# Linear attention and an ELU layer: two scratch buffers for the denominators' discarded products

## The chip, the cores and the metric

The kernel runs on one core of a Trainium2 chip. A core has five engines with a queue of instructions each: TensorE (PE in the profile; its loading of stationary weights is PEld), VectorE (DVE), ScalarE (ACT), GpSimd (POOL) and SyncE (SP), which here issues all the DMA transfers. Each engine works through its queue in the order in which it was written; across engines, and where one instruction has to see that an earlier one is through, semaphores hold an instruction back. The metric is the device time of one execution in microseconds; the median of several executions is given.

## The reference

```python
# q, k, v: (8, 8, 576, 64); omega: (128, 64), all float32
scale = 1 / sqrt(sqrt(64))
def phi(x):                                   # x already times scale
    proj = einsum('bhsd,md->bhsm', x, omega)
    h = proj - sum(x * x, axis=-1, keepdims=True) / 2
    return exp(h - max(h, axis=-1, keepdims=True)) / sqrt(128)
q_p, k_p = phi(q * scale), phi(k * scale)
kv  = einsum('bhsm,bhsd->bhmd', k_p, v)
z   = sum(k_p, axis=2)
num = einsum('bhsm,bhmd->bhsd', q_p, kv)
den = einsum('bhsm,bhm->bhs', q_p, z)[..., None] + 1e-6
x   = (num / den), laid out as 4608 tokens of 512
h   = x @ w_in                                # w_in (512, 2048), float64
g   = where(h > 0, h, exp(min(h, 0)) - 1)
out = (g @ w_out).astype(float32)             # w_out (2048, 512), float64
```

The change touches two things of it: how `den` is computed, and where two float32 copies of `omega` lie.

## The kernel before

The attention works on 32 pairs of heads (8 batches of 4 pairs). A pair is loaded (`load_pair`), its keys and queries are projected and exponentiated (`project`), the key-value product and the key sums are formed (`kv`), and `finish` divides the queries' features by the denominators and multiplies them by the key-value product. The first 8 pairs are "native": they are projected in float32 straight against a tile `of` of 128 x 128, whose upper half is omega transposed times -scale and whose lower half is a constant that multiplies the squares of x (line 491). The other 24 are split into a high and a low float32r part and projected against `om`, which is made once from a second float32 copy of omega, `omf` (lines 399 to 405).

The two layers behind the attention run beside it. The tokens go in blocks of 384 through `layer1` (lines 969 to 971) and `layer2` (lines 1003 to 1005), while the float64 weights are converted on VectorE, ScalarE and GpSimd (lines 891 to 923) in the first two hundred microseconds. The last 1536 tokens go through another, seven-product form (`wide1`, `wide2`) when the attention is over; its weights are prepared by `prepare` and `prepare2`.

All this is written as some thousands of tasks with an engine, an estimated duration, a due time, and the buffers each reads and writes (`Plan.op`). A planner (`Plan.order`) replays them by its own estimates, gives each engine the ready task with the earliest due time, and so fixes the order of the queues before anything runs. A `Buf` has a tag and a number of slots; buffers with one tag take turns in these slots, and the planner lets a task start only if a slot is free. On the chip, the first instruction that writes a buffer waits by semaphore until those that used its slot before are through.

The denominators of a pair are made in `finish` on VectorE, by lines 726 to 730: for each of 9 rows of 128 tokens, one `tensor_tensor_reduce` multiplies the query features by the key sums, which lie in PSUM as `pz`, and sums the product along its row into a column of `den`. The sum is all that is wanted; the product itself, 128 x 128 numbers, goes into a buffer `junk` that nobody reads. They come in three tasks per pair: two groups of four products, and a third one of two products on 64 partitions each (the ninth row belongs half to one head and half to the other). The planner counts 210 ns for each product. The profile shows one such product as two instructions, CUSTOM_DVE_ANT_0 and DVE_READ_ACCUMULATOR2_ANT. Line 555, in `project`, uses the same operation to add the two parts of a projection and take its minimum; its output is wanted and goes into different parts of the features `h`.

The buffer `junk` is a `Buf` with one slot, made anew for every product and not listed with the planner. The buffer for the key sums, tag `zs`, has one slot of 128 x 256 numbers. `omf` is in that slot first, and the sums of pairs 8 to 31 follow (lines 616 to 640). `of` has a place of its own for the whole kernel.

Of the kernel before, what the change touches and what calls it, by code (L numbers as in the profile page):

```python
# [9 lines left out]
F32 = mybir.dt.float32  # L10
# [8 lines left out]
P = 128  # L19
# [286 lines left out]
def act(n, psum=False, ptr=False):  # L306
    return (51 if psum else 93) + 0.833 * n + (93 if ptr else 0)
# [11 lines left out]
def performer_elu_kernel(  # L319
# [26 lines left out]
    make_identity(nc, ident)  # L346


    of = const.tile([P, M], F32, name="of")
    om = const.tile([P, 2 * M], F32R, name="om")  # L350
    nc.vector.memset(of[D:P], 0.5 * SCALE * SCALE)


    ones = const.tile([P, P], F32R, name="ones")
# [32 lines left out]
            nc.vector.tensor_scalar(x, x, -SCALE, None, ALU.mult)  # L387

    def omega(due):
        op("SP", 500, due + 0.005, lambda: nc.sync.dma_start(of[0:D], omT), (), ("of",), D * M * 4)  # L390
        op(
            "ACT", act(M), due + 0.1, lambda e: times(e, of[0:D]), ("of",), ("of",),
            alt=[("DVE", dve(M, True), 0.0)], port=True,
        )
        t = Buf(sb, [P, M], F32, "zs", "omf", 1)
        due += 15
        for a in range(2):
            r = slice(a * D, a * D + D)
            op("SP", 500, due, lambda r=r: nc.sync.dma_start(t()[r], omT), (), ((t, a),), D * M * 4)
        both = ((t, 0), (t, 1))  # L400
        op("ACT", act(M), due + 2, lambda e: times(e, t()), both, both, alt=[("DVE", dve(M, True), 0.0)], port=True)
        op("DVE", dve(M), due + 3, lambda: nc.vector.tensor_copy(om[:, 0:M], t()), ((t, 0), (t, 1)), ("oh",))
        op(
            "DVE", dve(M), due + 4,
            lambda: nc.vector.tensor_tensor(om[:, M:], t(), om[:, 0:M].bitcast(F32), ALU.subtract),
            ((t, 0), (t, 1), "oh"), ("om",),
        )
# [43 lines left out]
    def project(i, nm, due):  # L451

        s = st[i]
        x = s["x" + nm]
        h = s["h" + nm] = Buf(sb, [P, NJ, M], F32, "h", f"h{nm}_{i}", 4)
        nb = small("nb" + nm, NJ, f"nb{nm}_{i}")

        def exps(g, js, src, due, reads):
            def f():
                for j in js:  # L460
                    nc.scalar.activation(  # L461
                        h()[:, j, :], src(j), AF.Exp, bias=nb()[:, j:j + 1], scale=-1.0
                    )
            op("ACT", len(js) * act(M, native(i, nm), True), due, f, (*reads, (nb, g)), ((h, g),))

        if native(i, nm):
            for a in range(2):
                def square(e, a=a):
                    if e == "ACT":
                        nc.scalar.activation(x()[D:P, a], x()[0:D, a], AF.Square)  # L470
                    else:
                        tt(e, x()[D:P, a], x()[0:D, a], x()[0:D, a], ALU.mult)

                op(
                    "ACT", act(S), due - 3 + a, square, ((x, a),), ((x, a, 2),),
                    alt=other("sq", "POOL", pool(S), "DVE", dve(S)), port=True,
                )
            for g in range(3):
                d = due + 2.2 * g
                p = bank(i, "acc%d" % g, f"pp{nm}_{i}_{g}")  # L480
                n = 4 if g < 2 else 1
                js = slice(4 * g, 4 * g + n)

                def mms(g=g, p=p):
                    for c in range(4 if g < 2 else 2):
                        t, a = 2 * g + c // 2, c % 2
                        if g < 2:
                            o = p()[:, c * M:(c + 1) * M]
                        else:
                            o = p()[a * D:a * D + D, 0:M]  # L490
                        nc.tensor.matmul(o, x()[:, a, t * P:min(t * P + P, S)], of, start=True, stop=True)

                def view(p=p):
                    return p().rearrange("p (j x) -> p j x", j=4)

                op("PE", 872 if g < 2 else 240, d, mms, [*((x, a, 2) for a in range(2)), "of"], (p,))
                op(
                    "DVE", 66 + n * 133, d + 1,
                    lambda js=js, n=n, view=view: nc.vector.tensor_reduce(nb()[:, js], view()[:, 0:n], AX.X, ALU.min),
                    (p,), ((nb, g),),  # L500
                )
                exps(g, range(js.start, js.stop), lambda j, g=g, view=view: view()[:, j - 4 * g], d + 1.5, (p,))
            return

        def t():
            return x()[:, 1].rearrange("p (j d) -> p j d", d=D)

        op(
            "ACT", act(S), due - 4,
            lambda: nc.scalar.activation(t(), t(), AF.Square, scale=SCALE * 0.5**0.5), ((x, 3),), ((x, 3),),  # L510
        )
        sq = small("sq" + nm, NJ, f"sq{nm}_{i}")
        op("DVE", dve(S), due - 3, lambda: nc.vector.tensor_reduce(sq(), t(), AX.X, ALU.add), ((x, 3),), (sq,))

        y = Buf(sb, [P, 2 * S], F32R, "t", f"t{nm}_{i}", 2)
        for a in range(2):
            r, o = slice(a * D, a * D + D), slice(D - a * D, P - a * D)
            cs = slice(a * S, a * S + S)  # L520
            parts = ((x, 0),)
            op(
                "ACT", act(S), due - 5 + a, lambda e, r=r, cs=cs: copy(e, y()[r, cs], x()[r, 0]), parts, ((y, a, "h"),),
                alt=other("y_hi", "DVE", dve(S, True)), port=True,
            )
            op(
                "POOL", pool(S), due - 4 + a,
                lambda e, r=r, o=o, cs=cs: tt(e, y()[o, cs], x()[r, 0], y()[r, cs].bitcast(F32), ALU.subtract),
                (*parts, (y, a, "h")), ((y, a, "l"),), alt=other("y_lo", "DVE", dve(S)), port=True,
            )  # L530
        for c in range(5):
            d = due + 1.1 * c
            p = Buf(ps, [P, 512], F32, "pa", f"pp{nm}_{i}_{c}", 3)
            p2 = Buf(sb, [P, 2, M], F32, "p2", f"p2{nm}_{i}_{c}", 4)
            n = 2 if c < 4 else 1
            g = 0 if c < 2 else 1

            def mms(c=c, p=p, n=n):
                for a in range(n):
                    o = a * (S + D) + c * P  # L540
                    nc.tensor.matmul(p()[:, a * 256:(a + 1) * 256], y()[:, o:o + P], om, start=True, stop=True)  # L541

            def view(p=p):
                return p().rearrange("p (a x) -> p a x", a=2)

            op("PE", mm(256, n), d, mms, [(y, a, z) for a in range(2) for z in "hl"] + ["oh", "om"], (p,))
            op(
                "ACT", act(n * M, True), d + 0.5, lambda e, n=n, p2=p2, view=view: copy(e, p2()[:, 0:n], view()[:, 0:n, M:]),
                (p,), (p2,), alt=other("p2", "DVE", dve(n * M)),
            )  # L550

            def ttr(c=c, n=n, p2=p2, view=view):
                for a in range(n):
                    j = 2 * c + a
                    nc.vector.tensor_tensor_reduce(
                        out=h()[:, j, :], in0=view()[:, a, 0:M], in1=p2()[:, a, :], scale=1.0, scalar=LARGEST,
                        op0=ALU.add, op1=ALU.min, accum_out=nb()[:, j:j + 1],
                    )

            op("DVE", n * 212, d + 1, ttr, (p, p2), ((h, g, c), (nb, g, c)))  # L560
            if c in (1, 4):
                js = range(0, 4) if c == 1 else range(4, NJ)

                def bias(js=js):
                    m, q = nb()[:, js.start:js.stop], sq()[:, js.start:js.stop]
                    nc.gpsimd.tensor_tensor(m, m, q, ALU.add)
                    nc.gpsimd.tensor_tensor(m, m, q, ALU.subtract)  # L567

                op("POOL", 2 * pool(4), d + 1.3, bias, [sq, *((nb, g, e) for e in range(5))], ((nb, g),))
                exps(g, js, lambda j: h()[:, j, :], d + 1.5, [(h, g, e) for e in range(5)])  # L570
# [118 lines left out]
    def finish(i, due):  # L689
# [25 lines left out]
        for g in range(3):  # L715
# [7 lines left out]

            def dens(slots=slots):
                for j, a, r in slots:
                    junk = Buf(sb, [P, M], F32, "junk", f"junk_{i}_{j}_{a}", 1)
                    nc.vector.tensor_tensor_reduce(  # L727
                        out=junk()[r], in0=h()[r, j, :], in1=pz()[r, a * P:(a + 1) * P], scale=1.0, scalar=EPS,
                        op0=ALU.mult, op1=ALU.add, accum_out=den()[r, j:j + 1],
                    )  # L730
# [971 lines left out]
```

## Time and profile before

| | |
|---|---|
| median of 3 runs | 1024.42 us (1021.78 to 1025.25) |
| the profiled execution | 1023.41 us |
| its span, first to last instruction | 1021.6 us |
| granted TensorE clock, mean | 0.998 of full |
| TensorE, VectorE, ScalarE, GpSimd busy | 97%, 84%, 75%, 55% |
| denominators on VectorE (line 727, product) | 320 products, 90.4 us |
| their sums' reads (line 727) | 320, median 81 ns |

A busy TensorE is not TensorE at its peak, since matmuls are pipelined and their ends are modelled. Times of single instructions are in microseconds from the span's start. An engine's next instruction may start while the one before it is still on record, because the engine takes in new data while it is emptying; so the distance from start to start says what an instruction costs its queue, rather than its recorded duration. "Idle before" names what ended a wait, as inferred from the semaphores. The chain of waits follows the work that ended last back through what released each step.

### The profile page before, as it was taken

The numbers are of one execution on the slowest core, as the hardware profiler recorded it, in microseconds if no ns is written. First come the engines' busy times: TensorE is split into PE (matmuls) and PEld (weight loads), VectorE is DVE, ScalarE is ACT, GpSimd is POOL, SyncE is SP. The second block draws the span as 40 slices with busy tenths as digits, with TensorE's granted clock in tenths as the row PEclk, the third lists the DMA queues.
The fourth block names the chain that finished last, engine by engine and source line by source line (L and its number), as shares of the span: only waits on it lengthen the run. The fifth ranks groups of instructions, "written<-read, shape, count | busy, mean of one in ns | idle before, by whom it ended". The sixth has DMA issues, their size and how long they took to land.

```text
span 1021.6 us, 24319 instructions
## 1 busy us (share of the span) xinstructions
PE 988.5 (97%) x7806; PEld 887.3 (87%) x7806; DVE 856.6 (84%) x3077; ACT 767.9 (75%) x2064; POOL 559.0 (55%) x745
## 2 busy tenths in 40 slices
PE   8889999989999999999999999999999999999997
PEld 7777889878888888888888888887888999999997
DVE  5899978886778968887889888889999989779766
ACT  6888866876668888788887878785545788877774
POOL 1566666766546676676667776785442232223221
PEclk9999999999999999999999999999999999999999
DMA  7555777767766767676775767665787885775762
GB/s 201 153 178 187 231 254 256 243 213 240 238 218 222 231 203 229 200 229 198 245 227 183 238 194 234 203 224 209 261 306 275 304 294 176 237 235 193 229 198 70
DMA packets 93264, 226.27 MB, mean 221 GB/s; under 512 B 23056, under 2 KB 35024, under 8 KB 93136
## 3 DMA queue, kind: packets, MB, share of 16 engines
q1 hardware_dynamic: 93136, 224.70, 67.7%
q8 instruction: 63, 1.03, 0.4%
q14 instruction: 65, 0.53, 0.2%
HBM read 187.43 MB, written 37.22 MB: 220 GB/s over the span
## 4 chain that ended last, share of the span: by engine, by line
PE 64%; DVE 18%; ACT 7%; DMA 6%; issue 3%; POOL 1%; SPq 1%; DVEq 0%; ACTq 0%; POOLq 0%
PE acs L1512 8%; PE ph L969 6%; PE ph L971 6%; PE ph L970 6%; PE acc L1003 6%; PE A L1354 6%; PE acc L1005 6%; PE acc L1004 6%; PE B L1354 4%; DVE junk L727 3%; PE pkv L609 3%; PE ppq L541 2%; PE pn L829 2%; PE ppk L541 2%; DMA w1c<-w1s 1%
## 5 line engine op out<-in xcount | busy, mean ns | idle before, releaser
L969 PE MATMUL ph<-xh,w1c 128*128 128x384 f32 x512 | 177.2, 346 | 6.9 <-DVE g L990 4.9
L970 PE MATMUL ph<-xl,w1c 128*128 128x384 f32 x512 | 172.6, 337 | 1.2 <-DVE xl L794 1.2
L971 PE MATMUL ph<-xh,w1c 128*128 128x384 f32 x512 | 172.5, 337 | 0.0
L1003 PE MATMUL acc<-w2h,g 128*128 128x512 f32 x384 | 154.7, 403 | 0.1
L1005 PE MATMUL acc<-w2h,g 128*128 128x512 f32 x384 | 151.6, 395 | 0.0
L1004 PE MATMUL acc<-w2l,g 128*128 128x512 f32 x384 | 151.4, 394 | 0.0
L969 PEld LDWEIGHTS ph<-xh,w1c 128*128 128x128 f32 x512 | 96.4, 188 | 19.5 <-DVE g L990 9.7
L727 DVE CUSTOM_DVE_ANT_0 junk<-hq,pz 128x128 f32<-128x128 f32 (+1 forms) x320 | 90.4, 282 | 22.1 <-PE pz L705 10.3
L381 POOL TENSOR_TENSOR hq<-hq,den 128x512 f32<-128x512 f32 (+1 forms) x96 | 80.8, 850 | 36.6 <-DVE den L736 32.0
L970 PEld LDWEIGHTS ph<-xl,w1c 128*128 128x128 f32 x512 | 96.4, 188 | 4.2 <-DVE xl L794 1.6
L978 ACT ACTIVATE e<-ph 128x384 f32<-128x384 f32 x128 | 62.7, 489 | 47.3 <-PE ph L971 46.6
L971 PEld LDWEIGHTS ph<-xh,w1c 128*128 128x128 f32 x512 | 96.4, 188 | 0.0
L982 DVE SCALAR_TENSOR_TENSOR ph<-e,ph 128x384 f32<-128x384 f32 x128 | 71.2, 556 | 25.0 <-ACT e L979 24.2
L381 POOL TENSOR_TENSOR gq<-yh,gq 128x256 fp32r<-128x256 f32 x49 | 42.5, 868 | 86.5 <-ACT gq L376 76.3
L1005 PEld LDWEIGHTS acc<-w2h,g 128*128 128x128 f32 x384 | 72.1, 188 | 17.2
L1003 PEld LDWEIGHTS acc<-w2h,g 128*128 128x128 f32 x384 | 72.2, 188 | 16.0 <-issue 6.3
L381 POOL TENSOR_TENSOR tk<-xk,tk 64x576 fp32r<-64x576 f32 x45 | 64.1, 1425 | 31.8 <-ACT tk L376 16.8
L461 ACT ACTIVATE hq<-hq,nbq 128x128 f32<-128x128 f32 x216 | 68.5, 392 | 16.4 <-POOL nbq L567 16.0
L1004 PEld LDWEIGHTS acc<-w2l,g 128*128 128x128 f32 x384 | 72.3, 188 | 8.7
L461 ACT ACTIVATE hk<-hk,nbk 128x128 f32<-128x128 f32 x216 | 68.4, 392 | 15.0 <-POOL nbk L567 14.7
L381 POOL TENSOR_TENSOR tq<-xq,tq 64x576 fp32r<-64x576 f32 x46 | 65.8, 1431 | 19.6 <-ACT tq L376 8.2
L990 DVE TENSOR_TENSOR g<-ph,g 128x384 fp32r<-128x384 f32 x128 | 70.5, 550 | 6.0 <-PE pn L829 2.2
(222 smaller groups left out, 2827.3 us busy)
## 6 DMA issues: line engine op xcount, KB each, us to landing
w1c<-w1s SPq DMA_DIRECT2D x112, 512.0 KB, 4.4
wp<-w1t SPq DMA_DIRECT2D x48, 512.0 KB, 3.9
raw_w<-in_w_dram SPq DMA_DIRECT2D x32, 512.0 KB, 4.1
xk<-in_kx_dram SPq DMA_DIRECT2D x24, 576.0 KB, 4.5
xq<-in_qx_dram SPq DMA_DIRECT2D x24, 576.0 KB, 4.5
wp<-w1s SPq DMA_DIRECT2D x24, 512.0 KB, 4.1
v<-in_v_dram SPq DMA_DIRECT2D x32, 325.0 KB, 3.1
w1s<-w1c SPq DMA_DIRECT2D x16, 512.0 KB, 4.0
```

Of the source, the lines that this page charges most:

```text
L381: (nc.vector if e == "DVE" else nc.gpsimd).tensor_tensor(*args)
L461: nc.scalar.activation(h()[:, j, :], src(j), AF.Exp, bias=nb()[:, j:j + 1], scale=-1.0)
L727: nc.vector.tensor_tensor_reduce(out=junk()[r], in0=h()[r, j, :], in1=pz()[r, a * P:(a + 1) * P], scale=1.0, scalar=EPS, op0=ALU.mult, op1 ...
L969: nc.tensor.matmul(ph(), wh, xh[:, c, o:o + TB], start=(c == 0), stop=False)
L970: nc.tensor.matmul(ph(), wh, xl[:, c, o:o + TB], start=False, stop=False)
L971: nc.tensor.matmul(ph(), wl, xh[:, c, o:o + TB], start=False, stop=(c == NC - 1))
L982: lambda: nc.vector.scalar_tensor_tensor(ph(), e(), -1.0, ph(), ALU.add, ALU.max), (p, e), (p,),
L1003: nc.tensor.matmul(a(), g[0]()[:, ts], w2h[:, f], start=(f == f0), stop=False)
L1004: nc.tensor.matmul(a(), g[0]()[:, ts], w2l[:, f], start=False, stop=False)
L1005: nc.tensor.matmul(a(), g[1]()[:, ts], w2h[:, f], start=False, stop=(f == f1 - 1))
L1354: nc.tensor.matmul(o, at(a, i), u[b][:, i], start=(start and fresh_bank and i == 0 and n == 0), stop=(i == 1 and n == 2), skip_group_check ...
L1512: nc.tensor.matmul(bank()[:, z * TH:(z + 1) * TH], g()[:, a * TH + z * P:a * TH + z * P + P], w(b), start=(j == 0 and z == 0 and m == 0), ...
```

## The change

The buffer for the discarded products gets two slots instead of one, so that one product is written to one slot and the next to the other. The room for the second slot (512 bytes per partition) comes from `of`: it is no longer a place of its own but the first user of the key sums' slot, tag `zs`. `omf`, which was there before, takes one of the slots of `junk`. The tasks keep their engines, estimated durations and due times; `of` is named as a buffer to the planner where it was named by a string.

```diff
-    of = const.tile([P, M], F32, name="of")
+    of = Buf(sb, [P, M], F32, "zs", "of", 1)
     om = const.tile([P, 2 * M], F32R, name="om")
-    nc.vector.memset(of[D:P], 0.5 * SCALE * SCALE)
+    nc.vector.memset(of()[D:P], 0.5 * SCALE * SCALE)
...
     def omega(due):
-        op("SP", 500, due + 0.005, lambda: nc.sync.dma_start(of[0:D], omT), (), ("of",), D * M * 4)
+        op("SP", 500, due + 0.005, lambda: nc.sync.dma_start(of()[0:D], omT), (), (of,), D * M * 4)
         op(
-            "ACT", act(M), due + 0.1, lambda e: times(e, of[0:D]), ("of",), ("of",),
+            "ACT", act(M), due + 0.1, lambda e: times(e, of()[0:D]), (of,), (of,),
             alt=[("DVE", dve(M, True), 0.0)], port=True,
         )
-        t = Buf(sb, [P, M], F32, "zs", "omf", 1)
+        t = Buf(sb, [P, M], F32, "junk", "omf", 2)
...
-                        nc.tensor.matmul(o, x()[:, a, t * P:min(t * P + P, S)], of, start=True, stop=True)
+                        nc.tensor.matmul(o, x()[:, a, t * P:min(t * P + P, S)], of(), start=True, stop=True)
...
-                op("PE", 872 if g < 2 else 240, d, mms, [*((x, a, 2) for a in range(2)), "of"], (p,))
+                op("PE", 872 if g < 2 else 240, d, mms, [*((x, a, 2) for a in range(2)), of], (p,))
...
             def dens(slots=slots):
                 for j, a, r in slots:
-                    junk = Buf(sb, [P, M], F32, "junk", f"junk_{i}_{j}_{a}", 1)
+                    junk = Buf(sb, [P, M], F32, "junk", f"junk_{i}_{j}_{a}", 2)
                     nc.vector.tensor_tensor_reduce(
                         out=junk()[r], in0=h()[r, j, :], in1=pz()[r, a * P:(a + 1) * P], scale=1.0, scalar=EPS,
```

## Rows read from the trace of the kernel before

**Rows 1.** The page: busy us, share, instructions per engine; then the chain by engine.

```profile
PE 988.5 (97%) x7806; PEld 887.3 (87%) x7806; DVE 856.6 (84%) x3077; ACT 767.9 (75%) x2064; POOL 559.0 (55%) x745
...
PE 64%; DVE 18%; ACT 7%; DMA 6%; issue 3%; POOL 1%; SPq 1%; DVEq 0%; ACTq 0%; POOLq 0%
```

**Rows 2.** Stages: stretch, length; PE, PEld, DVE, ACT, POOL busy (instructions); clock, DMA.

```profile
22.00:125.00 103.00, 94.13 (x679) 78.65 (x679) 94.88 (x330) 87.93 (x237) 64.93 (x57) 1.00 0.60 189
125.00:300.00 175.00, 169.09 (x1091) 147.96 (x1091) 135.96 (x428) 124.95 (x303) 111.84 (x132) 1.00 0.71 234
300.00:725.00 425.00, 421.11 (x3620) 366.49 (x3618) 363.03 (x1690) 338.79 (x943) 294.62 (x448) 1.00 0.69 220
```

**Rows 3.** Chain of waits by line, 22 to 125 us, then 300 to 725 us.

```profile
by line: DVE junk L727 14.1%; issue 7.9%; DVE u_w L914 7.6%; DVE nbk L499 6.8%; ACT hq L461 5.7%; DVE u_w L902 5.6%; DVE nbq L499 5.2%; DVE u_w L909 5.1%; DVE xl L794 4.1%; DMA w1s<-w1c 3.8%; DVE qh L378 3.0%; DVE xq L381 2.5%; DVE ph L982 
...
by line: PE ph L969 10.1%; PE acc L1003 9.9%; PE ph L971 9.4%; PE ph L970 9.4%; PE acc L1005 9.3%; PE acc L1004 9.3%; PE pkv L609 5.4%; PE ppq L541 4.8%; PE pn L829 4.6%; PE ppk L541 4.0%; DVE junk L727 3.3%; DMA w1c<-w1s 1.9%; issue 1.4%; 
```

**Rows 4.** Line 727: duration min/median/max in ns, first and last start in us.

```profile
L727 DVE CUSTOM_DVE_ANT_0 junk<-hq,pz x320: 244/286/292, 22.6 to 724.2; 128x128 f32<-128x128 f32 x128, 64x128 f32<-64x128 f32 x32
...
L727 DVEq EVENT_SEMAPHORE  x31: 21/21/50, 23.0 to 111.3; - x31
```

**Rows 5.** VectorE in order of time from 404.5 us: start, duration, line, operation.

```profile
404.52 0.29 DVE L727 CUSTOM_DVE_ANT_0 junk<-hq,pz 128x128 f32<-128x128 f32 x1 [1.75 <-PE pz L705]
404.74 0.08 DVE L727 DVE_READ_ACCUMULATOR2_ANT den<- 128x1 f32 x1
404.85 0.29 DVE L727 CUSTOM_DVE_ANT_0 junk<-hq,pz 128x128 f32<-128x128 f32 x1
...
405.73 0.08 DVE L727 DVE_READ_ACCUMULATOR2_ANT den<- 128x1 f32 x1
405.73 0.28 DVE L555 CUSTOM_DVE_ANT_0 hq<-ppq,p2q 128x128 f32<-128x128 f32 x1
...
405.94 0.28 DVE L555 CUSTOM_DVE_ANT_0 hq<-ppq,p2q 128x128 f32<-128x128 f32 x1
```

**Rows 6.** VectorE in order of time from 88.3 us, a native pair's denominators.

```profile
88.36 0.08 DVE L727 DVE_READ_ACCUMULATOR2_ANT den<- 128x1 f32 x1
88.58 0.29 DVE L727 CUSTOM_DVE_ANT_0 junk<-hq,pz 128x128 f32<-128x128 f32 x1
```

**Rows 7.** VectorE in order of time from 69.9 us, a pair's third group.

```profile
69.93 0.07 DVE L727 DVE_READ_ACCUMULATOR2_ANT den<- 64x1 f32 x1
70.04 0.29 DVE L727 CUSTOM_DVE_ANT_0 junk<-hq,pz 64x128 f32<-64x128 f32 x1
70.26 0.08 DVE L727 DVE_READ_ACCUMULATOR2_ANT den<- 64x1 f32 x1
70.37 0.69 DVE L499 TENSOR_REDUCE nbq<-ppq 128x4 f32<-128x512 f32 x1
```

**Rows 8.** Stages, line 727 alone: stretch, length, VectorE busy (records of two instructions).

```profile
22.00:125.00 103.00, 23.25 (x160) 1.00 0.60 189
...
300.00:725.00 425.00, 60.93 (x420) 1.00 0.69 220
```

**Rows 9.** ScalarE's waits, 22 to 125 us: waiter, releaser, us in total, times, longest.

```profile
ACT hk L461 <- DVE nbk L499: 6.8, 7, 1.6
```

**Rows 10.** Users of the moved buffers: duration in ns, first and last start in us.

```profile
L491 PE MATMUL ppq<-of,xq x160: 272/275/377, 18.2 to 110.7; 128*128 128x128 f32 x128, 128*64 128x128 f32 x32
...
L405 DVE TENSOR_TENSOR om<-omf,om x1: 282/282/282, 16.0 to 16.0; 128x128 fp32r<-128x128 f32 x1
...
L625 POOL TENSOR_TENSOR zs<-hk x24: 725/738/1140, 138.2 to 689.1; 128x256 f32<-128x256 f32 x24
```

**Rows 11.** Weight loads: issues of the page (us to landing); chain; TensorE behind it.

```profile
w1c<-w1s SPq DMA_DIRECT2D x112, 512.0 KB, 4.4
...
718.18 8.04 DMA w1c<-w1s
...
726.36 0.41 PE L969 MATMUL ph<-xh,w1c 128*128 128x384 f32 x1 [1.53 <-DMA w1c<-w1s]
```

## The prediction

> **What bounds the kernel now.** I read the page first, then a table of busy time by stage, then the chain of waits in the same stages, and last the order of single VectorE instructions. The page shows TensorE busy for 97% of the span and VectorE for 84%, while the chain that ended last runs 18% of the span through VectorE [rows 1]. Line 727 computes the denominators. The averages hide that there are three regimes [rows 2]. From 22 to 125 us (eight "native" pairs beside the weight conversion) TensorE is idle for 8.9 of 103 us, and VectorE's recorded 94.9 us leave out its short pauses between denominators. From 125 to 300 us TensorE is idle for 5.9 of 175 us, and from 300 to 725 us for 3.9 of 425. Line 727 works from 22.6 us [rows 4] to 725 us and nowhere behind that. The chain of waits gives line 727 14.1% of the first stretch, more than any other line, and 3.3% of 300 to 725 [rows 3]. So the change acts on the resource that sets the first stage, and on one that sets the end only now and then afterwards.
>
> **What one denominator costs.** A product is two instructions, the product itself and the read of its sum. In a group of four, products start at 404.52, 404.85 and so on, one every 0.33 us; each begins 0.11 us after the read ahead of it began, and the last read at 405.73 has line 555 behind it starting at the same moment [rows 5]. Line 555 is the same operation on the same shape, but writes a different part of its result each time: its products start 0.21 us apart, 405.73 to 405.94, with none of that pause. The pause thus belongs not to the operation and not to what follows a denominator; it stands between two products that write the one junk buffer. With two buffers a product waits for the product before the last. In these rows the successor could start 0.33 us after the start of the one it waited for; at a pitch of 0.21 the next but one starts after 0.42. That leaves 0.09 us, so I take the whole 0.12 us as gone. The bounds are 0 (the wait only moves to another place) and 0.12 us; I take the upper, as the row of line 555 is the same instruction.
>
> **How many.** 32 pairs with two groups of four: 32 x 2 x 3 = 192 products with one of their own group ahead, and 192 x 0.12 = 23.0 us of VectorE time, 48 x 0.12 = 5.8 us of it in the native pairs. In some native pairs a product waits for something else too, and a separate wait instruction stands ahead, 31 times [rows 4]; there the next product starts 0.22 us behind the read, not 0.11 [rows 6]. With its condition long true that instruction can run beside the product ahead, so 31 x 0.11 = 3.4 us more, bounds 0 and 3.4. The third group of a pair is two products of 64 rows: the second starts 0.11 us after the first one's read, but line 499 behind it, which does not touch the buffer, starts 0.11 us late as well [rows 7]. What holds those is not the buffer, and I count none of these 32 (the other bound: 32 x 0.11 = 3.5 us). The Trainium skill has a rule for it, in "VectorE: DVE Perf Modes", section "Two Vector instructions with no wait between them": an instruction whose output starts in another group of 32 partitions than the last output waits for all earlier ones. By it the third group keeps its pause with any number of buffers; the rows agree with it.
>
> VectorE so loses 5.8 + 3.4 = 9.2 us of work and pauses before 125 us, and 144 x 0.12 = 17.3 us later: 26.5 us in all.
>
> **What of it is on the path.** In the first stretch the chain holds 14.1% x 103 = 14.5 us of line 727, whose busy time there is 23.25 us [rows 3, 8]: 62%. 0.62 x 9.2 = 5.7 us is the most that this stage can give. What is late next is ScalarE, busy for 87.9 us of the 103 [rows 2], but 6.8 us of its idle time in this stretch is itself a wait for line 499 on VectorE [rows 9], so it follows VectorE forward. TensorE's idle 8.9 us also has to yield the gain. I take 4 of 5.7. From 300 to 725 the chain holds 3.3% x 425 = 14.0 us of 60.93 us [rows 3, 8], 23%; 420 of the 480 records of these 24 pairs lie there, so 17.3 x 420/480 x 0.23 = 3.5 us at most. TensorE has only 3.9 us idle there, and not all of it behind a denominator, so I take 2. From 125 to 300 lie 60 records and no term: bounds 0 and 17.3 x 60/480 = 2.2 us. After 725 nothing changes; that stretch starts earlier. Sum: 4 + 2 = 6 us.
>
> **The moved copies of omega.** Nothing is added: the same instructions, SP's three loads of omega included, with the same planned durations and due times. The first copy now holds the key sums' buffer until the last native projection has read it. That read starts at 110.7 us; the first key sum, on GpSimd, starts at 138.2 [rows 10]: 27 us of room, so it costs nothing and gives the planner no reason to reorder. If that cover were gone, the first pair's key sums would wait on GpSimd, with the other subtractions behind them. The second copy now takes a junk buffer; its last reader, line 405, starts at 16.0 us [rows 10], 6.6 us ahead of the first product, on the same engine. Both at 0. Below nothing is excluded for the dependencies by these margins; for the different place in memory no row gives a bound, and I take 0.
>
> **The sum.** The profiled execution took 1023.41 us, 1.8 us more than its span, and lies 1.0 us under the median of 1024.42. 1023.41 - 6 = 1017.4 by it, 1018.4 by the median; I write 1018.0.
>
> **Rivals.**
> - *The chain gives back all of it*, and pauses outside its rows too: 5.7 + 3.5 + up to 2.2 = 9.2 to 11.4 us, 1012 to 1015. For it: every piece after 125 us is started by something earlier, so a shift passes on. Against it: ScalarE and TensorE at 85 and 91% in the first stretch [rows 2].
> - *Hidden.* TensorE and ScalarE take over in the first stage as soon as VectorE is some per cent faster, and the later pieces lie beside a full TensorE. Then 1 to 3 us come, 1021 to 1023. For it: TensorE's 421 of 425 us. Against it: the chain's rows.
> - *Nothing is removed.* The pause is VectorE emptying behind each product, whatever the buffer, and the time stays at 1023.4 to 1024.4. For it: each pause follows one instruction of the same kind. Against it: rows 5, line 555. The Trainium skill gives this rule in "VectorE: DVE Perf Modes", section "The DRAIN you can't avoid": the emptying cannot be skipped by leaving semaphores out, and "the semaphore costs nothing extra here". By it the sum would be 0; this trace disagrees, with 0.33 us against 0.21.
> - *Slower.* The place is the end of the attention, where loads and stores crowd SP's queue: a weight load issued at 718.18 takes 8.04 us where such loads land in 4.4, and TensorE then stands for 1.53 us [rows 11]. If a faster VectorE bunches the stores ahead of such loads, each load that comes as late costs up to 8.04 - 4.4 = 3.6 us. Two eat up the gain; from the third on the kernel is slower: 1018 + 3 x 3.6 = 1029. Against it: one such wait of TensorE stands in the rows, and the order of the queue is unchanged.
>
> **How the numbers follow.** Main case (4 to 8 us gone, 1016 to 1020) 0.55; all given back 0.16; hidden 0.17; nothing removed 0.06; slower 0.06. A range that leaves out under 2 in 10 goes from 1012.5 into the hidden and the unchanged case: 1012.5 to 1024.0. A difference under 0.3% (3.1 us) can't be told from no change here; faster means under 1021.3. Main and full cases and a third of the hidden one make faster 0.77, the rest of it and the empty one same 0.17, slower 0.06.
>
> **What would show it.** In the changed kernel's order of VectorE instructions, products of a group of four 0.21 to 0.22 us apart, the 64-row ones with their 0.11 us kept; the separate waits without a pause behind them; line 727's idle time, beside its waits for line 705, near nothing. The last native projection starts some 4 us before 110.7 us, the last product some 6 us before 725, and the stretch behind it keeps its 297 us. Wrong: a pitch still at 0.33 (the wait is not the buffer's); or a pitch of 0.21 with line 727's rows gone from the chain and TensorE's or ScalarE's in their place at the same total (hidden); or a first key sum that waits for line 491.

## The result and the profile after

The changed kernel takes 1008.16 us (median of 4, 1005.99 to 1008.90) against 1023.10 (median of 4, 1020.72 to 1025.25): ratio 0.985, with a 95% interval of 0.982 to 0.988. In a second set of runs it is 0.986 (0.983 to 0.989). That is 15 us, where 6 were forecast, and below the range of 1012.5 to 1024.0. The order of the instructions is the same on all five engines.

The page after, its first and its chain line:

```profile
PE 981.2 (97%) x7806; PEld 883.9 (88%) x7806; DVE 842.0 (84%) x3077; ACT 765.8 (76%) x2064; POOL 557.6 (55%) x745
...
PE 68%; DVE 15%; DMA 6%; ACT 5%; issue 3%; POOL 3%; SPq 1%; DVEq 0%; POOLq 0%; ACTq 0%
```

VectorE after, the same four products as in [rows 5] and line 555 behind them (start, duration, line, operation):

```profile
392.93 0.29 DVE L727 CUSTOM_DVE_ANT_0 junk<-hq,pz 128x128 f32<-128x128 f32 x1 [1.73 <-PE pz L705]
393.15 0.08 DVE L727 DVE_READ_ACCUMULATOR2_ANT den<- 128x1 f32 x1
393.15 0.28 DVE L727 CUSTOM_DVE_ANT_0 junk<-hq,pz 128x128 f32<-128x128 f32 x1
...
393.56 0.28 DVE L727 CUSTOM_DVE_ANT_0 junk<-hq,pz 128x128 f32<-128x128 f32 x1
393.77 0.08 DVE L727 DVE_READ_ACCUMULATOR2_ANT den<- 128x1 f32 x1
393.77 0.29 DVE L555 CUSTOM_DVE_ANT_0 hq<-ppq,p2q 128x128 f32<-128x128 f32 x1
```

Each product now starts together with the read ahead of it, 0.21 us apart: the pause is gone. A native pair shows 0.21 to 0.22 us as well, against 0.44 before [rows 6 show its pause of 0.22], and its separate wait instructions, 23 now for 31, cost 0.02 us at most:

```profile
20.35 0.08 DVE L727 DVE_READ_ACCUMULATOR2_ANT den<- 128x1 f32 x1
20.35 0.28 DVE L727 CUSTOM_DVE_ANT_0 junk<-hq,pz 128x128 f32<-128x128 f32 x1
20.56 0.08 DVE L727 DVE_READ_ACCUMULATOR2_ANT den<- 128x1 f32 x1
20.57 0.29 DVE L727 CUSTOM_DVE_ANT_0 junk<-hq,pz 128x128 f32<-128x128 f32 x1
```

The third group keeps a pause, 0.08 us ahead of its second product and 0.11 behind it, where before 0.11 and 0.11 stood [rows 7]:

```profile
62.79 0.07 DVE L727 DVE_READ_ACCUMULATOR2_ANT den<- 64x1 f32 x1
62.87 0.29 DVE L727 CUSTOM_DVE_ANT_0 junk<-hq,pz 64x128 f32<-64x128 f32 x1
63.09 0.08 DVE L727 DVE_READ_ACCUMULATOR2_ANT den<- 64x1 f32 x1
63.20 0.69 DVE L499 TENSOR_REDUCE nbq<-ppq 128x4 f32<-128x512 f32 x1
```

Summed over all products that have another one just ahead, the time from the start of the read to the start of the next product falls from 30.3 us to 3.2. VectorE has lost 27.1 us, for which 26.5 were counted.

The stages after. The windows are laid so that each holds the same work as its counterpart in [rows 2]: 330 VectorE, 237 ScalarE and 57 GpSimd instructions in the first.

```profile
19.00:115.00 96.00, 93.22 (x677) 78.38 (x678) 91.09 (x330) 88.00 (x237) 65.29 (x57) 1.00 0.65 204
115.00:290.00 175.00, 170.07 (x1095) 148.38 (x1094) 134.07 (x428) 124.90 (x304) 111.86 (x133) 1.00 0.71 234
290.00:709.00 419.00, 416.82 (x3619) 365.94 (x3617) 354.96 (x1690) 337.10 (x939) 292.42 (x447) 1.00 0.70 223
```

The first stage takes 96 us for 103. TensorE's idle time in it falls from 8.9 us to 2.8, while ScalarE's busy time stays at 88: the others follow VectorE. The middle stage keeps its 175 us. The third takes 419 for 425. Line 727 falls from 14.1% of the first stage's chain [rows 3] to 6.6%, and in the third stage it is no longer among the lines that the view prints (chain by line, first stage, then third):

```profile
by line: DVE u_w L914 7.9%; DVE junk L727 6.6%; PE ppq L491 6.4%; DVE nbk L499 6.0%; DVE u_w L902 5.5%; issue 5.2%; DVE u_w L909 4.7%; DMA xq<-in_q_dram 3.9%; PE ppk L491 3.7%; PE pkv L665 3.6%; DVE qh L378 3.4%; ACT hq L461 3.3%; DVE xl L7
...
by line: PE acc L1003 11.0%; PE ph L969 11.0%; PE acc L1005 10.4%; PE ph L971 10.4%; PE ph L970 10.3%; PE acc L1004 10.3%; PE pkv L609 5.7%; PE ppq L541 5.1%; PE pn L829 4.9%; PE ppk L541 4.1%; DMA xq<-in_qx_dram 1.4%; DMA xk<-in_kx_dram 1.
```

The starts of the same TensorE instruction in both profiles say where the 15 us lie. How much earlier it starts in the changed kernel, its lead, in us (the upper row is the time in the kernel before):

```
time in the kernel before    20     140     300     690     705    1000
lead                        2.9    10.0    10.4    13.4    15.7    15.1
```

So 7.1 us come in the native stage, 3.0 from 300 to 690 us, and two pieces were not in the sum at all: 2.9 us before the first product has begun, and 2.3 us between 690 and 705.

The first piece is TensorE's rate. The same first projections after the pause at 10 us take 3.79 us in the kernel before (0.24 us per record) and 2.19 us after (0.14). Kernel before, then after:

```profile
11.57 3.79 PE L491 MATMUL ppk<-of,xk 128*128 128x128 f32 x16 [1.65 <-ACT hk L461]
```

```profile
11.30 2.19 PE L491 MATMUL ppk<-of,xk 128*128 128x128 f32 x16 [1.44 <-ACT hk L461]
```

The second piece is mostly the granted clock, which is 0.53, all but its lower level of 1.2 GHz, from 700 to 702 us in the kernel before, behind 2 us in which TensorE was busy for 0.52; the record has it low for 3.4 us in all. In the changed kernel TensorE pauses in the same place and the clock stays at 2.4 GHz. Columns as in [rows 2]; kernel before, then after:

```profile
698.00:700.00 2.00, 0.52 (x10) 0.55 (x12) 1.97 (x10) 0.00 (x0) 0.00 (x0) 1.00 0.64 260
700.00:702.00 2.00, 2.00 (x18) 1.67 (x15) 1.58 (x10) 1.18 (x4) 1.62 (x5) 0.53 0.00 0
```

```profile
684.00:686.00 2.00, 0.65 (x12) 0.68 (x14) 1.97 (x10) 0.00 (x0) 0.00 (x0) 1.00 1.00 404
686.00:688.00 2.00, 2.00 (x21) 1.78 (x17) 2.00 (x11) 1.31 (x5) 1.75 (x5) 1.00 0.07 25
```

### The profile page after: what moved, and what is told of

The parts are those of the page before. It is cut to its first block, busy times and chain, and to the rows that moved or that the text cites. A ratio compares the mean times of both kernels' runs of the same rounds, so it can differ in the third digit from the quotient of the medians.

```text
span 1006.4 us, 24315 instructions
## 1 busy us (share of the span) xinstructions
PE 981.2 (97%) x7806; PEld 883.9 (88%) x7806; DVE 842.0 (84%) x3077; ACT 765.8 (76%) x2064; POOL 557.6 (55%) x745
## 4 chain that ended last, share of the span: by engine, by line
PE 68%; DVE 15%; DMA 6%; ACT 5%; issue 3%; POOL 3%; SPq 1%; DVEq 0%; POOLq 0%; ACTq 0%
PE acs L1512 9%; PE ph L969 6%; PE ph L971 6%; PE acc L1003 6%; PE ph L970 6%; PE A L1354 6%; PE acc L1005 6%; PE acc L1004 6%; PE B L1354 4%; PE pkv L609 2%; PE pn L829 2%; PE ppq L541 2%; PE ppk L541 2%; DVE junk L727 1%; DVE u_w L914 1%
## 5 line engine op out<-in xcount | busy, mean ns | idle before, releaser
L969 PEld LDWEIGHTS ph<-xh,w1c 128*128 128x128 f32 x512 | 96.2, 188 | 18.7 <-DVE g L990 8.5
L727 DVE CUSTOM_DVE_ANT_0 junk<-hq,pz 128x128 f32<-128x128 f32 (+1 forms) x320 | 74.6, 279 | 12.7 <-PE pz L705 10.6
L461 ACT ACTIVATE hk<-hk,nbk 128x128 f32<-128x128 f32 x216 | 68.4, 391 | 15.7 <-POOL nbk L567 15.3
```

The source lines that it names most:

```text
L461: nc.scalar.activation(h()[:, j, :], src(j), AF.Exp, bias=nb()[:, j:j + 1], scale=-1.0)
L727: nc.vector.tensor_tensor_reduce(out=junk()[r], in0=h()[r, j, :], in1=pz()[r, a * P:(a + 1) * P], scale=1.0, scalar=EPS, op0=ALU.mult, op1 ...
L969: nc.tensor.matmul(ph(), wh, xh[:, c, o:o + TB], start=(c == 0), stop=False)
```

## The experiments

The expectations name the theories by letters. A: the waits that are gone are the cause. B: the new places of omega's copies are. C: the path as predicted, with its discounts. D: the later gain is hidden. E: the change raises the granted clock. Each edit is shown against the changed kernel; the idle matmuls go into the kernel before as well.

**The kernel before once more.** No edit.

> The kernel before once more, for a second profile of it. In the first one TensorE's granted clock reached full only at 17.45 us, in the changed kernel's at 9.37 us, and 2.9 us of the difference between the two profiles lie there, ahead of the first denominator. Theory A (waits): the clock's rise comes at a time of its own in each execution, so here it may come anywhere from some 6 to 20 us, the span follows it by up to 3 us, and the median stays within 0.3% of 1023. Theory B (places): the rise belongs to the kernel, since omega's copies lie elsewhere; then it is late here again, at 17 to 18 us.

1023.78 us, ratio to the kernel before 0.998 (0.996 to 1.001). TensorE's early rate is another one than in the first profile: the first 20 projection records take 2.42 us, where they took 4.41 in the first profile; then TensorE stands for 4.84 us, and the clock is at half from 12 to 18.7 us.

```profile
12.00:14.00 2.00, 1.19 (x5) 1.20 (x6) 1.97 (x4) 2.00 (x8) 0.00 (x0) 0.50 1.03 421
14.00:16.00 2.00, 2.00 (x12) 2.00 (x11) 1.08 (x4) 1.06 (x4) 0.00 (x0) 0.50 0.56 159
```

At 700 us this execution has no drop. So both pieces of clock differ from one execution of the same kernel to the next; neither comes with the kernel every time.

**Omega's copies moved, one junk buffer.**

```diff
-        t = Buf(sb, [P, M], F32, "junk", "omf", 2)
+        t = Buf(sb, [P, M], F32, "junk", "omf", 1)
...
-                    junk = Buf(sb, [P, M], F32, "junk", f"junk_{i}_{j}_{a}", 2)
+                    junk = Buf(sb, [P, M], F32, "junk", f"junk_{i}_{j}_{a}", 1)
```

> Omega's two copies moved as in the change, but one junk buffer, so every product waits for the one ahead as before. Theory A (waits): no change, ratio 0.998 to 1.002, products of a group still 0.33 us apart. Theory B (places): the early rise of the clock and its 3 us come with the places, ratio about 0.997, and the rise stands near 9 us.

1023.34 us, ratio 0.999 (0.996 to 1.001); the pause between products is 0.12 us as before. The places are worth nothing that these runs can tell. Its profiled execution was a long one, span 1026.5 us, and shows what the clock can cost: it fell five times ahead of the end, once behind two windows in which TensorE was busy for 1.2 of 2 us each (columns as in [rows 2]):

```profile
26.00:28.00 2.00, 1.18 (x11) 1.04 (x10) 1.91 (x8) 0.98 (x4) 0.42 (x1) 1.00 0.95 310
28.00:30.00 2.00, 1.16 (x8) 0.97 (x8) 1.93 (x7) 1.45 (x6) 1.99 (x2) 1.00 0.67 180
30.00:32.00 2.00, 1.80 (x9) 1.80 (x10) 1.23 (x4) 1.82 (x6) 0.75 (x2) 0.55 0.01 4
32.00:34.00 2.00, 2.00 (x13) 1.45 (x13) 1.33 (x2) 1.24 (x6) 0.00 (x0) 0.60 0.00 0
```

**Two buffers for the native pairs alone.** The others all write one and the same buffer.

```diff
+        same = st.setdefault("same", Buf(sb, [P, M], F32, "junk", "junk_same", 2))
...
-                    junk = Buf(sb, [P, M], F32, "junk", f"junk_{i}_{j}_{a}", 2)
+                    junk = Buf(sb, [P, M], F32, "junk", f"junk_{i}_{j}_{a}", 2) if i < NSWAP else same
```

> Two junk buffers for the denominators of pairs 0 to 7, one and the same buffer for pairs 8 to 31; omega's copies as in the change. Theory A (waits): the gain of the first stage alone, 6 to 8 us by the two profiles (6.9 us between 20 and 125 us), ratio 0.992 to 0.994. Rival C (path as predicted): 4 us, at most 5.7, ratio 0.9945 to 0.996. Theory B (places) adds 3 us to either.

1014.45 us, ratio 0.990 (0.9875 to 0.9925). The native stage takes 96.0 us again, with the same 330 VectorE instructions:

```profile
21.30:117.30 96.00, 93.14 (x677) 78.32 (x678) 91.11 (x330) 87.96 (x237) 65.32 (x57) 1.00 0.65 203
```

**Two buffers for the later pairs alone.** The same line with `if i >= NSWAP`.

> One and the same junk buffer for pairs 0 to 7, two for pairs 8 to 31; omega's copies as in the change. Theory A (waits): the gain of the later stages alone, 3.5 to 6 us (3.7 us between 125 and 690 us in the two profiles, and perhaps the 1.7 us of a clock drop at 700 us that the changed kernel did not have), ratio 0.994 to 0.9965. Rival C (path as predicted): 2 us, ratio 0.998. Rival D (hidden): within 0.2% of before, the later gain exists only behind the earlier one.

1017.37 us, ratio 0.993 (0.991 to 0.996). Its native stage is that of the kernel before, 103.0 us:

```profile
22.00:125.00 103.00, 94.21 (x679) 78.72 (x680) 95.06 (x330) 87.93 (x237) 65.00 (x57) 1.00 0.61 189
```

There are six pairs of profiles in which one kernel has the waits in the native pairs and the other has not: the kernel before, its repetition and this one, each against the changed kernel and the part experiment above. (The profile with the moved copies alone is left out, for its clock falls three times in this stretch.) The lead between 20 and 140 us grows by 6.9 to 7.1 us in every one. That is the native term by the traces: 7.0 us, from 9.1 us of VectorE time. Between the instructions that start at 250 and at 690 us in the kernel before, it grows by 2.4 to 3.8 us over the pairs in which only one of the two has the later waits: the later term by the traces, about 3.

The times say more than the traces do. The two ratios, 0.990 and 0.993, are both below what theory A named (0.992 to 0.994 and 0.994 to 0.9965). Part of that is the clock: its mean over the runs is 0.9934 in the kernel before of this set, 0.9968 and 0.9960 in the part experiments. Against runs of kernels that all wait, at the same mean clock (the straight line that the next experiment describes), the native pairs alone gain 8.0 us and the later ones alone 5.3, each known to some 1.5 us by the spread of its 6 or 7 runs. Their sum is 13.3, and the changed kernel, taken in the same way, gains 13.6: the two terms add up. So C's 4 (at most 5.7) for the native pairs and its 2 for the later ones do not stand, and the later gain does not need the earlier one (D). Of theory A the cause stands, and its native 6 to 8 us; its later 3.5 to 6 us fit the times and not quite the traces.

**The changed kernel once more.** No edit.

> The changed kernel once more. In its first profile TensorE's clock was full from 9.37 us on; in the five other profiles so far (two of the kernel before, three partial ones) it was full for good only from 16.5 to 18.7 us, and 2 to 4 us lie there. Theory A (waits and, apart from them, the clock): the trace path gives 7.0 us in the native stage and 4 us later, 11 us; the early clock was luck, so here it is full for good only at 16 to 19 us in the profile, and the ratio is 0.986 to 0.990. Theory E (the change brings the clock): TensorE's shorter pauses let the clock drop less often in every execution, so the ratio stays at 0.983 to 0.987 and the mean granted clock of the runs stays above that of the kernel before on the same chip.

1008.60 us, ratio 0.986 (0.983 to 0.989). The clock was up early again, against theory A, and the ratio lies where the two theories meet. The runs' mean granted clock tells more. Over 86 timed executions of kernels whose products all wait it averages 0.9945, over 10 of the changed kernel 0.9976, and in the 86 a straight line through time and clock has 7.6 us per 0.01. 0.0031 x 760 = 2.4 us of the 15 go with the clock: an estimate by that line, which fits theory E, on the average and beside the waits. That TensorE's shorter pauses are what raises it fits the rows, but no run changed these pauses alone.

**Idle matmuls in TensorE's first pause**, in the changed kernel and in the kernel before.

```diff
+                    if (i, nm, g) == (0, "k", 2): [nc.tensor.matmul(idle()[:, 0:P], ident, ident, start=True, stop=True) for idle in [Buf(ps, [P, 512], F32, "ph", "idle", 2)] for _ in range(4)]
```

> The changed kernel, with four idle matmuls on TensorE behind the first projection of pair 0's keys, where it stands for 1.7 to 2.6 us in all profiles (from about 9.8 us on) and the clock falls to half afterwards in four of six. They write a bank that nobody reads. Clock theory: without that pause the clock stays up, the profile shows it full from about 10 us at the latest with no drop before 20 us, and 2 to 4 us come off: ratio 0.002 to 0.004 below the changed kernel's of this call. Rival (the pause is not what the clock goes by): no change beside it, or up to 0.4 us slower.

> The kernel before with the same four idle matmuls. Clock theory: 2 to 4 us faster than before, ratio 0.996 to 0.998, with later drops of the clock (behind TensorE's pauses at 26, 97 and 130 us, and at 700 us) as frequent as ever. Rival: ratio 0.999 to 1.001.

1007.78 us, ratio 0.986 (0.983 to 0.989), beside 0.986 of the changed kernel on the same chip, and 1023.14 us, ratio 0.9995 (0.9975 to 1.0015). Both profiles have the clock up from 9.7 and 9.9 us, without a drop before 20 us, as the clock theory has it (in the kernel before it falls later, at 27 and 99 us); but the times show nothing of the 2 to 4 us. A miss: most executions may have the early rise without the filling too, or the filling does not bring it, or what it brings is lost again behind it. Which of these stays open.

**More VectorE work in the native stage.**

```diff
-                for j, a, r in slots:
+                for j, a, r in slots + slots * (i < NSWAP and slots[0][0] == 0):
```

> The changed kernel with 32 + 0 needless products put back: in each native pair the four products of the first group are made twice (same numbers, same columns), 8 x 4 x 0.21 = 6.7 us more VectorE work before 125 us, none of it waiting. Theory A (VectorE sets the native stage, ScalarE and TensorE only follow it): the stage loses what it gained per unit of VectorE time, 7.0/9.1 = 0.77, so 5 us; the lead of the changed kernel over this one grows by 4.5 to 6 us between 20 and 125 us, ratio to the changed kernel 1.005. Rival C (the prediction's discount: with the waits gone ScalarE and TensorE are next and VectorE has slack): at most 0.4 of it, 1 to 3 us.

1014.45 us, ratio to the kernel before 0.991 (0.988 to 0.993), some 5 us over the changed kernel's 0.986. In the traces the changed kernel's lead over it grows by 4.4 us between 20 and 140 us: 0.66 of the 6.7 us put in, just under the lower end of A and above all of C. The native stage takes 100 us for 96 (columns as in [rows 2]):

```profile
22.00:122.00 100.00, 93.90 (x676) 78.22 (x677) 96.11 (x393) 87.79 (x237) 64.53 (x57) 1.00 0.62 194
```

So after the change, too, VectorE's work sets most of the native stage's length.

**One product for the ninth row, native pairs.**

```diff
+            for a in range(2):
+                nc.tensor.matmul(pz()[a * D:a * D + D, 2 * P:3 * P], z()[:, a:a + 1].to_broadcast([P, D]), ident, start=True, stop=True)
...
-                slots = [(8, a, slice(a * D, a * D + D)) for a in range(2)]
+                slots = [(8, a, slice(a * D, a * D + D)) for a in range(2)] if i >= NSWAP else [(8, 2, slice(0, P))]
...
-            op("DVE", len(slots) * 210, d, dens, (hg, pz), ((den, g),))
+            op("DVE", max(len(slots), 2) * 210, d, dens, (hg, pz), ((den, g),))
```

> The changed kernel, native pairs only: the ninth row's two products on 64 partitions become one on 128, for which TensorE spreads the key sums of both heads into a third block of the same bank (two matmuls of 64 columns more per pair, some 0.2 us). VectorE loses 8 x (0.21 + 0.09) = 2.4 us. Theory A (VectorE sets the native stage): 1.5 to 2.2 us off between 20 and 125 us in the traces, less up to 0.5 us for TensorE's additions; in the times, ratio 0.998 to the changed kernel, hardly told from none. Rival C (VectorE no longer sets it): 0 to 0.5 us, or slower by TensorE's 1.6 us.

1013.33 us, ratio to the kernel before 0.990 (0.988 to 0.993): some 4 to 5 us slower than the changed kernel (0.985 and 0.986). In the traces 1.6 us of that arise between 20 and 140 us and 2.1 between 300 and 690, where the two kernels do the same work; the latter is not explained, and it says how far the later leads of single profiles can be trusted. The 1.6 us are a miss for theory A, which had 1.5 to 2.2 us off, and what rival C named in its second half (slower by TensorE's 1.6 us). TensorE's addition, priced at 0.2 us per pair, puts off the next matmul by 0.27 us, and it stands ahead of the products, which wait for `pz`:

```profile
19.54 0.44 PE L710 MATMUL pz<-ident,z 128*64 128x128 f32 x4
19.81 0.39 PE L491 MATMUL ppk<-of,xk 128*64 128x128 f32 x4
```

So TensorE's work counts in the native stage after the change, beside VectorE's; this run took from one engine and added to the other, and does not tell the two shares apart. No version was found that beats the changed kernel.

## Why the prediction was wrong

- *The pause, and how much of it goes: right.* 0.33 to 0.21 us in groups of four, 0.44 to 0.22 in native pairs, 27.1 us in all for 26.5. Two buffers suffice, and the separate waits run beside the product ahead. The pause goes with the wait for the instruction just ahead, and not with writing one place twice, for it stands where nothing is written twice too: line 378 waits for line 982 just ahead, whose result it reads, and starts 0.66 us behind it; line 555, which reads other data, starts 0.46 us behind the same line (kernel before):

```profile
399.98 0.56 DVE L982 SCALAR_TENSOR_TENSOR ph<-e,ph 128x384 f32<-128x384 f32 x1 [1.17 <-ACT e L979]
400.64 0.56 DVE L378 CAST g<-ph 128x384 fp32r<-128x384 f32 x1
...
406.15 0.56 DVE L982 SCALAR_TENSOR_TENSOR ph<-e,ph 128x384 f32<-128x384 f32 x1
406.61 0.28 DVE L555 CUSTOM_DVE_ANT_0 hq<-ppq,p2q 128x128 f32<-128x128 f32 x1
```

- *The third group keeps its pause: right.* In both part experiments, where the two halves write different rows of the one buffer, no wait on it stands between them, and the second still starts 0.09 us late. The Trainium skill's rule ("VectorE: DVE Perf Modes", section "Two Vector instructions with no wait between them") agrees: the output starts in another group of partitions.
- *"I take 4 of 5.7": this step failed first.* It discounted the native stage because ScalarE and TensorE would be late next. They were not: 103 us became 96, TensorE's idle 8.9 us became 2.8, ScalarE's busy time did not change, and the native pairs gave 7.0 us by the traces and 8.0 by the times. The last native projection starts 9.0 us earlier, at 101.7 us, and not some 4; 2.9 of that are the early clock. The bound of 5.7 was itself too low. The chain is one path; from 22 to 50 us of the kernel before it ran over ScalarE's line 461 for 24% and over line 727 for only 10, and I read that share as if the other VectorE work there were free. From 50 to 100 us VectorE shed 3.3 us of pauses and the stage 3.5.
- *"I take 2" of 3.5 later: too small.* About 3 by the traces (2.4 to 3.8), 5.3 by the times at equal clock. So some 2 us of the later term are not placed. They may lie between 200 and 220 us, where two executions of the changed kernel differ by 2.5 us (from 195 to 222 us of its own time, TensorE waits 2.6 us for VectorE's line 990 in one and 0.3 in the other), and between 690 and 726; that was not settled.
- *The clock: missing from the sum, so put at nothing without a reason.* By the line through 86 executions it is worth 2.4 us on the average. TensorE's pauses of over 0.9 us from start to start between 22 and 125 us go from seven to none, and the clock falls behind some such pauses, not all. The mean of 0.998 and the rows of 1.00 did not show it: the first 17 us, in which a projection record took 0.24 us and not 0.14, are not in that number.
- Together: by the traces 7.0 + 3 and by the line 2.4 make 12.4 us; by the times 8.0 + 5.3 + 2.4 make 15.7, where 15 were measured (12 to 18 by the interval).
- *Moved copies of omega: right*, 0.999 (0.996 to 1.001); the first key sum starts 26.5 us behind the last native projection instead of 27.5.
- *Rivals.* "Nothing is removed" fell: 0.44 us against 0.22 on the same instruction and data. So did the Trainium skill's rule behind it ("VectorE: DVE Perf Modes", section "The DRAIN you can't avoid"): here a wait for the instruction just ahead costs 0.12 us. "Hidden" fell by the native part experiment's 7.0 us and by the added products. The slower case did not occur. "All given back", with 9.2 to 11.4 us, was the nearest, and still short.

## What to carry to other kernels

Look for an engine that waits for itself: two neighbours of one instruction, the one with a pause behind each predecessor and the other without, and ask which buffer they share. A discarded output is a buffer like any other, and one that turns with a second costs only its room. Where one engine is busy for nearly all of a stage and the others follow it, take most of what it sheds (here 7.0 us of 9.1, and 4.4 of 6.7 put back), not the share of the chain that one line holds.

## What was not expected of the hardware

- A wait instruction of its own ahead of the product costs as much again as the wait inside it (0.22 us from read to next product against 0.11) while its condition is late, and 0 to 0.02 us when it is met early.
- With the mean granted clock of a run the time changes by 7.6 us per 0.01 (a straight line through 86 executions), and executions of the kernel before lie between 0.987 and 1.000. The part of a run before the clock's first rise does not enter it.
- Not every pause of TensorE brings the clock down: 0.65 us busy of 2 was followed by 1.00, 0.52 of 2 by 0.53.
